# Joining three float32 words of a float64 weight: the sign by a one-operand 16-bit AND, and the last tile's output in halves

## The chip, the cores and the metric

One core of one Trainium2 chip. The metric is the device time of one execution in microseconds (us); the time before is the median of three timed runs.

## The reference

Three parts follow one another; here they are, cut to what is computed (`silu(g) = g * sigmoid(g)`):

```python
# 1: chunked state-space attention: batch 4, heads 8, sequence 768, head dim 32, state 16
for c in chunks:
    L = exp(cum[i] - cum[j]) * (i >= j)
    y = ((C @ B.T) * L) @ x + (C @ state) * exp(cum)
    state = decay_full * state + sum_j(B_j x_j * decay_from_j)
# 2: gated feed-forward, 3072 tokens x 256, inner width 1536
xn = x / sqrt(mean(x * x) + 1e-6) * rms_g
x2 = (silu(xn @ w_gate) * (xn @ w_val)) @ w_out
# 3: token-shift feed-forward, inner width 1024
xk = mu_k * x2 + (1 - mu_k) * x2_prev;  xr = mu_r * x2 + (1 - mu_r) * x2_prev
out = sigmoid(xr @ w_r) * (relu(xk @ w_k) ** 2 @ w_v)
```

The weights come as float64. The kernel does the matrix products with float32r operands in two parts: a rounded high part and the residual, three matmuls for one product.

## The kernel before, in words

The 768 positions are cut into six tiles of 128; with four batches a tile is 512 columns (T = 512). Tile t goes through attention of chunk t, then the normalization, then `ffn1` (twelve units u of 128 inner columns), then `mix`, then `ffn2` (eight units). The stages of neighbouring tiles are interleaved by `hook`: during `ffn1` of tile t (kind "ab") the attention of chunk t + 1 is put between the units, its decay exponentials (`exp_e`, for chunks 0 and 1 on ScalarE) or scans (`e_scan` L410, VectorE) before them; during `ffn2` of tile t - 1 (kind "cd") the normalization of chunk t + 1.

`mm3` (L623) issues three matmuls into one PSUM bank: high weight and high x, low weight and high x, high weight and low x. `split` (L126) makes the two parts of an activation: a cast on ScalarE (L128) and a subtraction on VectorE (L131). In `ffn1` a unit is g, v (L641, L644), a silu on ScalarE (L655), the product hf on VectorE (L656), its split, and two units later `contract` into two accumulators, one for each half of 128 output channels.

**Weights.** 27 pieces (`wjobs`) of 128 x 512 float64 are loaded two at a time into a staging buffer `wst` (two buffers, L238, SP queue) and converted by `convert` (L245), for two pieces in 1024 columns (the last one alone, 512): fourteen steps. A float64 lies there as two 32-bit words, low `lo` and high `hi`. ScalarE scales the high word, read as float32, into `t` (L257), and turns the low word into its top three bits as a number from 0 to 7, in place (L258). VectorE clamps `t` (L262). Then come the two joins in `merge`, each with two operands: `hi = (t AND sign) OR lo` (L267), and `t = (t << 3) OR hi` (L269). `parts` casts `t` to the high part on ScalarE (L278) and subtracts for the low one on VectorE (L279). The first two steps run after the normalization of chunk 0 in program order, the others when `need` asks for them: in `ffn1` of tile 0 by the list NEED, then one a unit in tile 1.

**The end.** `ffn2` contracts unit u three units late (`contract`, L705, both halves m for each unit), so after the gate's matmuls `rps` and its sigmoid three units are left (L736), then for each half one product (L739) and one store of 256 KB (L740).

**The order.** The program order is not the issue order. `arrange` (L1129) takes all instructions, prices each (`price`, L998: a VectorE instruction with two operands at 1.03 ns a column, with one at 0.52, plus 75), finds what depends on what by address ranges (`region` L979, `meet` L991, with a marker for the even or odd place of a stride of two), and simulates a list schedule: an engine that is free takes the ready instruction that stands first in the program. That order is then fixed on each engine, the SP and ScalarE queues' DMA issues among them.

Of the kernel before, what the change touches and what calls it, by code (L numbers as in the profile page):

```python
# [8 lines left out]

F32 = mybir.dt.float32  # L10
F32R = mybir.dt.float32r
BF16 = mybir.dt.bfloat16
I32, U32 = mybir.dt.int32, mybir.dt.uint32
AF = mybir.ActivationFunctionType
ALU = mybir.AluOpType
# [3 lines left out]
NC = S // P  # L19
DM, DFF, DFF2 = 256, 1536, 1024  # L20
NU, NK = DFF // P, DFF2 // P
T = NB * P
# [27 lines left out]
TOP3 = (2.0 ** -29 * (1 - 2.0 ** -12), 7.5 * 2.0 ** -12 - 0.5)  # L50
# [17 lines left out]
def tile_kernel(ctx: ExitStack, tc, a_c, x_t, B_t, B_s, C_s, B_p, C_p, C_h, kc,  # L68
                w_gate, w_val, w_out, w_k, w_v, w_r, out):
    nc = tc.nc  # L70
# [21 lines left out]
    def t2(name, dt=F32, tag="t2"):  # L92
        return rp.tile([P, T], dt, tag=tag, bufs=5, name=name)

    def t4(name, dt=F32, tag="wt"):
        return rp.tile([P, 2, T], dt, tag=tag, bufs=1, name=name)
# [3 lines left out]
    def pair(tag, name, dt=F32R):  # L100
        return rp.tile([P, 2, T], dt, tag=tag, bufs=pair_bufs[tag], name=name)
# [4 lines left out]
    def f32(ap):  # L106
        return ap.bitcast(F32)
# [29 lines left out]
    RE = 2 * 2 * NB  # L137
    starts = t2("starts", BF16)[:RE].rearrange("p (h i) -> p h i", h=4)
    nc.gpsimd.memset(starts, 1.0)
# [3 lines left out]
    for base in (0, -32):  # L143
        nc.gpsimd.affine_select(out=pick, in_=f32(pick), pattern=[[-1, RE]], base=base, channel_multiplier=1,
                                compare_op=ALU.not_equal, fill=1.0)
    eye = wp.tile([P, P], BF16, name="eye")
    before = wp.tile([P, P], BF16, name="before")
    nc.gpsimd.memset(eye, 0.0)
# [4 lines left out]
                            compare_op=ALU.is_ge, fill=-30000.0)  # L153
    cmask = wp.tile([P, NH * P], BF16, name="cmask")
    nc.gpsimd.memset(cmask, 0.0)
    nc.gpsimd.affine_select(out=cmask, in_=cmask, pattern=[[0, NH], [1, P]], base=0, channel_multiplier=-1,
                            compare_op=ALU.not_equal, fill=1.0)
    lmask = wp.tile([P, NB, P + 1], BF16, name="lmask")
    nc.gpsimd.memset(lmask, 0.0)
# [41 lines left out]
    def wpair(k, m, name):  # L201
        return (wp.tile([P, k, m], F32R, name=name + "h"), wp.tile([P, k, m], F32R, name=name + "l"))

    wg, wv, wo = wpair(2, DFF, "wg"), wpair(2, DFF, "wv"), wpair(NU, DM, "wo")
    wk, wvv, wr = wpair(2, DFF2, "wk"), wpair(NK, DM, "wvv"), wpair(2, DM, "wr")
# [10 lines left out]
    for q in range(NU // 2):  # L216
        s, k2 = slice(2 * P * q, 2 * P * (q + 1)), slice(2 * q, 2 * q + 2)
# [10 lines left out]
    staged = {}  # L228
# [15 lines left out]

    def convert(j):  # L245
        js = range(j, min(j + 2, len(wjobs)))
        st = staged.pop(j // 2).rearrange("p i a b -> p (i a b)").rearrange("p (n w) -> p n w", w=2)
        t2w = t4("wt2", I32, "Cs" if j % 4 else "wt")
        tw = t2w.rearrange("p i n -> p (i n)")

        def part(i):
            s = slice(0, T * len(js)) if i is None else slice(T * i, T * i + T)
            return st[:, s, 0], st[:, s, 1], tw[:, s]

        def magnitude(i=None):
            lo, hi, t = part(i)
            nc.scalar.activation(out=t.bitcast(F32), in_=hi.bitcast(F32), func=AF.Copy, scale=2.0 ** -112)  # L257
            nc.scalar.activation(out=lo, in_=lo.bitcast(U32), func=AF.Copy, scale=TOP3[0], bias=TOP3[1])  # L258

        def move(i=None):  # L260
            lo, hi, t = part(i)
            nc.vector.tensor_scalar(out=t.bitcast(F32), in0=t.bitcast(F32), scalar1=-W_MAX, scalar2=W_MAX,  # L262
                                    op0=ALU.max, op1=ALU.min)

        def merge(i=None):
            lo, hi, t = part(i)
            nc.vector.scalar_tensor_tensor(out=hi, in0=t, scalar=-0x80000000, in1=lo,  # L267
                                           op0=ALU.bitwise_and, op1=ALU.bitwise_or)
            nc.vector.scalar_tensor_tensor(out=t, in0=t, scalar=3, in1=hi,  # L269
                                           op0=ALU.logical_shift_left, op1=ALU.bitwise_or)  # L270

        def parts(i=None):
            for n, k in enumerate(js):
                if i not in (None, n):
                    continue
                _, wh, wl = wjobs[k]
                t = t2w[:, n, :].rearrange("p (k m) -> p k m", k=2).bitcast(F32)
                nc.scalar.copy(wh, t)  # L278
                (vec_e if k in SUB_DVE else pool_e).tensor_tensor(out=wl, in0=t, in1=f32(wh), op=ALU.subtract)  # L279

        return magnitude, move, merge, parts

    done = [0, 0]
# [418 lines left out]
    def ffn2(t, hook):  # L702
        acc = [None, None]
        hs = {}

        def contract(u):
            h = hs.pop(u)
            for m in range(2):
                if u == 0:
                    acc[m] = patt.tile([P, T], F32, tag="at", name=f"v_{m}")  # L710
                mm3(acc[m], wvv, u, m, h, u == 0, u == NK - 1)

        for u in range(NK):
            hook("cd", u)
            kp = pmm.tile([P, T], F32, tag="mm", name="kp")
            for k in range(2):
                mm3(kp, wk, k, u, xm[t, 0, k], k == 0, k == 1)
            if u == 0:
                hook("cd2", u)
            rl, k2 = t2("rl"), t2("k2")  # L720
            nc.scalar.activation(out=rl, in_=kp, func=AF.Relu)  # L721
            nc.vector.tensor_mul(k2, rl, rl)  # L722
            hs[u] = pair("hl", "h2")
            split(hs[u], k2, act_e, vec_e)
            if u >= 3:
                contract(u - 3)
        hook("cd", NK)
        rs = []
        for m in range(2):
            rps = pmm.tile([P, T], F32, tag="mm", name="rps")  # L730
            for k in range(2):
                mm3(rps, wr, k, m, xm[t, 1, k], k == 0, k == 1)
            r = t2("r")
            tabled(out=r, in_=rps, func=AF.Sigmoid)
            rs.append(r)
        for u in range(NK - 3, NK):  # L736
            contract(u)
        for m in range(2):
            nc.vector.tensor_mul(rs[m], rs[m], acc[m])  # L739
            nc.sync.dma_start(out=out[t, m], in_=rs[m])  # L740


    full, cols = slice(0, T), (slice(0, T // 2), slice(T // 2, T))
# [67 lines left out]
    for t in range(NC):  # L811
        c, e = t + 1, t + 2
# [127 lines left out]
class Order:  # L940
# [37 lines left out]
    @staticmethod  # L978
    def region(a, slots):  # L979
        ap = a.bass_ap  # L980
        steps = list(ap.ap)
        row = max(1, steps[0][0])
        at = ap.offset % row
        if ap.tensor.name.startswith("la_") or slots.get(ap.tensor.name, ("",))[0] == "PSUM":
            return ap.tensor.name, (0, 1 << 40, 0, P, None)
        end = at + sum((c - 1) * max(s, 0) for s, c in steps[1:]) + 1
        size = 2 if ap.tensor.dtype == BF16 else 4
        return ap.tensor.name, (at * size, end * size, ap.offset // row, ap.offset // row + steps[0][1],
                                at % 2 if steps[-1][0] == 2 else None)

# [186 lines left out]
```

## Time and profile before

| | |
|---|---|
| median of three timed runs | 533.19 us (532.39 to 533.31) |
| the profiled execution | 534.13 us |
| its span, first to last instruction | 532.1 us |
| mean granted TensorE clock | 0.994 of full speed |
| busy, TensorE matmul | 517.5 us (97%) |
| busy, VectorE | 402.7 us (76%) |
| busy, ScalarE | 314.7 us (59%) |
| busy, GpSimd | 14.3 us (3%) |

The page gives the busy time of each engine over the whole span. A table by stage gives the same for a stretch, with the granted clock. A group of instructions gives the mean duration of one and the time that the engine idled just before them, with what ended that idle time. L267 is line 267 of the kernel. PE is TensorE's matmuls, PEld its weight loads, DVE is VectorE, ACT ScalarE, POOL GpSimd, SP the engine that issues most transfers (SPq and ACTq are the queues of issues).

### The profile page before, as it was taken

To read this page: it belongs to the slowest core of one execution; us is meant where nothing else is said; L and a number is where in the kernel's file an instruction comes from. 1 tells how busy PE (TensorE), PEld (TensorE's weight loads), DVE (VectorE), ACT (ScalarE), POOL (GpSimd) and SP (SyncE) were. 2 spreads that over 40 slices of the span, in tenths; PEclk is the share of its full clock that TensorE was granted. 3 is DMA by queue.
4 is the path that set the end of the run, shared out by engine and by line. 5 is a ranking of instruction groups with operands and counts; after the bars stand their busy time and mean duration, and the time that the engine had idled before them with its cause. 6 is when DMAs were issued, how large, how long until landed. Compare 5 with 4: busy or idle time off the path is not lost.

```text
span 532.1 us, 7505 instructions
## 1 busy us (share of the span) xinstructions
PE 517.5 (97%) x2831; PEld 414.7 (78%) x2831; DVE 402.7 (76%) x640; ACT 314.7 (59%) x546; POOL 14.3 (3%) x30
## 2 busy tenths in 40 slices
PE   9969989999989999999999999999999999999997
PEld 6646767778768888888788888888888888888885
DVE  5798999999999986587996598986455863335772
ACT  4998768845736774445774445774437663245552
POOL 4000000000002000001000001000000000000000
PEclk9988999999999999999999999999999999999999
DMA  8543565534334011314011314011000010000001
GB/s 256 196 158 112 172 216 183 173 94 149 99 109 149 20 41 41 118 62 176 22 39 42 119 58 160 1 41 39 1 0 2 2 39 1 0 0 1 21 21 39
DMA packets 21635, 42.20 MB, mean 79 GB/s; under 512 B 2064, under 2 KB 4880, under 8 KB 21600
## 3 DMA queue, kind: packets, MB, share of 16 engines
q1 hardware_dynamic: 19296, 33.34, 18.8%
q10 hardware_dynamic: 2304, 8.39, 4.7%
q8 instruction: 22, 0.36, 0.3%
q14 instruction: 13, 0.11, 0.1%
HBM read 38.38 MB, written 3.34 MB: 78 GB/s over the span
## 4 chain that ended last, share of the span: by engine, by line
PE 89%; DVE 2%; ACT 2%; DMA 1%; issue 1%; ACTq 0%; DVEq 0%
PE v L625 10%; PE v L627 10%; PE v L626 10%; PE g L625 7%; PE g L626 6%; PE x L627 6%; PE g L627 6%; PE x L625 6%; PE x L626 6%; PE kp L625 4%; PE kp L627 4%; PE kp L626 4%; PE y L494 2%; PE y L523 1%; PE sc L462 1%; PE rps L626 1%
## 5 line engine op out<-in xcount | busy, mean ns | idle before, releaser
L656 DVE TENSOR_TENSOR hf<-sl,v 128x512 f32<-128x512 f32 x72 | 49.2, 683 | 48.8 <-PE v L627 45.2
L128 ACT CAST h<-hf 128x512 fp32r<-128x512 f32 x72 | 44.5, 618 | 62.7 <-DVE hf L656 58.5
L116 ACT ACTIVATE sl<-g 128x512 f32<-128x512 f32 x72 | 42.7, 593 | 44.5 <-PE g L627 44.4
L131 DVE TENSOR_TENSOR h<-hf,h 128x512 fp32r<-128x512 f32 x72 | 50.4, 702 | 23.4 <-ACT h L128 23.3
L625 PE MATMUL g<-xn,wgh 128*128 128x512 f32 x144 | 58.4, 409 | 1.5 <-ACT sl L116 0.8
L625 PE MATMUL x<-h,woh 128*128 128x512 f32 x144 | 56.5, 393 | 0.8 <-ACT h L128 0.8
L626 PE MATMUL g<-xn,wgl 128*128 128x512 f32 x144 | 57.2, 397 | 0.0
L625 PE MATMUL v<-xn,wvh 128*128 128x512 f32 x144 | 56.4, 395 | 0.6 <-ACT sl L116 0.6
L627 PE MATMUL g<-xn,wgh 128*128 128x512 f32 x144 | 56.9, 395 | 0.0
L626 PE MATMUL v<-xn,wvl 128*128 128x512 f32 x144 | 56.5, 392 | 0.0
L627 PE MATMUL v<-xn,wvh 128*128 128x512 f32 x144 | 56.3, 391 | 0.0
L627 PE MATMUL x<-h,woh 128*128 128x512 f32 x144 | 55.8, 391 | 0.4 <-DVE h L131 0.4
L626 PE MATMUL x<-h,wol 128*128 128x512 f32 x144 | 56.1, 389 | 0.0
L722 DVE TENSOR_TENSOR k<-rl 128x512 f32<-128x512 f32 x48 | 35.2, 738 | 15.1 <-ACT rl L721 14.9
L128 ACT CAST h<-k 128x512 fp32r<-128x512 f32 x48 | 29.7, 620 | 16.0 <-DVE k L722 15.9
L131 DVE TENSOR_TENSOR h<-k,h 128x512 fp32r<-128x512 f32 x48 | 32.7, 685 | 7.4 <-ACT h L128 7.0
L721 ACT ACTIVATE rl<-kp 128x512 f32<-128x512 f32 x48 | 28.4, 595 | 16.2 <-PE kp L627 15.8
L625 PE MATMUL kp<-xm,wkh 128*128 128x512 f32 x96 | 37.8, 393 | 0.0
L627 PE MATMUL v<-h,wvvh 128*128 128x512 f32 x96 | 37.5, 390 | 0.0
L627 PE MATMUL kp<-xm,wkh 128*128 128x512 f32 x96 | 37.5, 390 | 0.0
L625 PE MATMUL v<-h,wvvh 128*128 128x512 f32 x96 | 37.4, 389 | 0.0
L626 PE MATMUL v<-h,wvvl 128*128 128x512 f32 x96 | 37.4, 389 | 0.0
(135 smaller groups left out, 1040.7 us busy)
## 6 DMA issues: line engine op xcount, KB each, us to landing
E<-la_r ACTq DMA_DIRECT2D x16, 512.0 KB
x<-in_x_t SPq DMA_DIRECT2D x6, 512.0 KB
wst<-in_w_gate SPq DMA_DIRECT2D x6, 512.0 KB
wst<-in_w_val SPq DMA_DIRECT2D x6, 512.0 KB
wst<-in_w_out SPq DMA_DIRECT2D x6, 512.0 KB
Br<-in_B_s SPq DMA_DIRECT2D x12, 256.0 KB
Cr<-in_C_s SPq DMA_DIRECT2D x12, 256.0 KB
out<-r SPq DMA_DIRECT2D x12, 256.0 KB
```

Of the source, the lines that this page charges most:

```text
L116: ins.append(lambda: nc.scalar.activation(out=out, in_=in_, func=func, **kw))
L128: nc.scalar.copy(x[:, 0, :], src)
L131: last[0] = le.tensor_tensor(out=x[:, 1, :], in0=src, in1=f32(x[:, 0, :]), op=ALU.subtract).ins
L462: nc.tensor.matmul(bank[half][:, q * 256:(q + 1) * 256], bs[:, p, :], cs[:, p, :, :].rearrange("p a i -> p (a i)"), start=True, stop=True)
L494: nc.tensor.matmul(y[half][32 * j:32 * j + 32, at[half]:at[half] + P], x[:, b, h * D:(h + 1) * D], m[:, h, :], start=start and at[half] == ...
L523: mm = nc.tensor.matmul(y[half][:, k * P:(k + 1) * P], Sf[g, b + k].rearrange("p h d -> p (h d)"), d["Ch"][g, b + k, :], start=k == 0, sto ...
L625: nc.tensor.matmul(ps, w[0][:, k, ws], x[:, 0, :], start=first, stop=False)
L626: nc.tensor.matmul(ps, w[1][:, k, ws], x[:, 0, :], start=False, stop=False)
L627: nc.tensor.matmul(ps, w[0][:, k, ws], x[:, 1, :], start=False, stop=last)
L656: nc.vector.tensor_mul(hf, sl, v)
L721: nc.scalar.activation(out=rl, in_=kp, func=AF.Relu)
L722: nc.vector.tensor_mul(k2, rl, rl)
```

## The change

The first join is replaced. ScalarE's second pass (L258) writes its 0 to 7 as a 16-bit number over the lower half of the high word (whose value the first pass has read by then). VectorE takes the upper half of `t`, as 16-bit numbers, ANDs it with 0x8000 and writes it to the upper half of the high word: one operand and a constant. So the high word then holds sign and low bits, and the second join is as before.

In the last tile the three remaining contractions are done for half 0 of the output first, then for half 1, and half 1's product and store are cut in two of 256 columns.

The planner's `region` knows the 16-bit type.

```diff
-BF16 = mybir.dt.bfloat16
+BF16, U16 = mybir.dt.bfloat16, mybir.dt.uint16
     def convert(j):
         js = range(j, min(j + 2, len(wjobs)))
-        st = staged.pop(j // 2).rearrange("p i a b -> p (i a b)").rearrange("p (n w) -> p n w", w=2)
+        sf = staged.pop(j // 2).rearrange("p i a b -> p (i a b)")
+        st = sf.rearrange("p (n w) -> p n w", w=2)
...
+        def halves(i):
+            s = slice(0, T * len(js)) if i is None else slice(T * i, T * i + T)
+            h = sf.bitcast(U16).rearrange("p (n w) -> p n w", w=4)[:, s]
+            return h[:, :, 2], h[:, :, 3]
+
         def magnitude(i=None):
             lo, hi, t = part(i)
             nc.scalar.activation(out=t.bitcast(F32), in_=hi.bitcast(F32), func=AF.Copy, scale=2.0 ** -112)
-            nc.scalar.activation(out=lo, in_=lo.bitcast(U32), func=AF.Copy, scale=TOP3[0], bias=TOP3[1])
+            nc.scalar.activation(out=halves(i)[0], in_=lo.bitcast(U32), func=AF.Copy, scale=TOP3[0], bias=TOP3[1])
...
         def merge(i=None):
             lo, hi, t = part(i)
-            nc.vector.scalar_tensor_tensor(out=hi, in0=t, scalar=-0x80000000, in1=lo,
-                                           op0=ALU.bitwise_and, op1=ALU.bitwise_or)
+            nc.vector.tensor_scalar(out=halves(i)[1], in0=t.bitcast(U16).rearrange("p (n w) -> p n w", w=2)[:, :, 1],
+                                    scalar1=0x8000, scalar2=None, op0=ALU.bitwise_and)
             nc.vector.scalar_tensor_tensor(out=t, in0=t, scalar=3, in1=hi,
                                            op0=ALU.logical_shift_left, op1=ALU.bitwise_or)
...
-        for u in range(NK - 3, NK):
-            contract(u)
+        if t + 1 < NC:
+            for u in range(NK - 3, NK):
+                contract(u)
+        else:
+            us = [(u, hs.pop(u)) for u in range(NK - 3, NK)]
+            for m in range(2):
+                for u, h in us:
+                    mm3(acc[m], wvv, u, m, h, False, u == NK - 1)
         for m in range(2):
-            nc.vector.tensor_mul(rs[m], rs[m], acc[m])
-            nc.sync.dma_start(out=out[t, m], in_=rs[m])
+            parts = [slice(0, T)] if m == 0 or t + 1 < NC else [slice(0, T // 2), slice(T // 2, T)]
+            for c in parts:
+                nc.vector.tensor_mul(rs[m][:, c], rs[m][:, c], acc[m][:, c])
+                nc.sync.dma_start(out=out[t, m][:, c], in_=rs[m][:, c])
...
-        size = 2 if ap.tensor.dtype == BF16 else 4
+        size = 2 if ap.tensor.dtype in (BF16, U16) else 4
```

## Rows read from the trace of the kernel before

**Rows 1.** The page's busy line: busy us (share of span) and instructions.

```profile
PE 517.5 (97%) x2831; PEld 414.7 (78%) x2831; DVE 402.7 (76%) x640; ACT 314.7 (59%) x546; POOL 14.3 (3%) x30
```

**Rows 2.** The table by stage; columns as in its first line.

```profile
core 0: us, PE busy (x) PEld busy (x) DVE busy (x) ACT busy (x) POOL busy (x), PEclk, DMA share, GB/s
24.70:31.00 6.30, 1.68 (x8) 0.69 (x7) 5.88 (x14) 6.10 (x19) 0.00 (x0) 1.00 0.70 221
31.00:34.20 3.20, 3.20 (x8) 2.21 (x9) 3.20 (x7) 3.20 (x7) 0.00 (x0) 0.50 0.02 6
34.20:44.20 10.00, 8.45 (x36) 5.45 (x34) 9.96 (x16) 9.76 (x30) 0.00 (x0) 0.99 0.61 212
44.20:48.70 4.50, 4.45 (x12) 3.51 (x13) 2.67 (x5) 3.78 (x6) 0.00 (x0) 0.62 0.33 101
...
78.00:80.30 2.30, 0.88 (x6) 0.79 (x5) 2.06 (x7) 2.27 (x7) 0.00 (x0) 1.00 1.00 319
80.30:146.40 66.10, 66.06 (x424) 51.93 (x422) 65.21 (x99) 45.62 (x73) 0.11 (x1) 1.00 0.42 138
146.40:151.00 4.60, 2.88 (x11) 1.67 (x11) 4.60 (x8) 2.26 (x5) 0.00 (x0) 1.00 0.35 96
151.00:528.20 377.20, 377.19 (x1979) 310.71 (x1979) 263.82 (x422) 205.28 (x337) 7.43 (x6) 1.00 0.13 46
```

**Rows 3.** Groups by line and shape: busy us, mean ns; then L267 alone in one stage.

```profile
L412 DVE TENSOR_TENSOR_SCAN E<-E,cmask 128x1024 f32<-128x1024 f32 x16 | 36.6, 2285 | 0.9 <-DMA E<-la_r 0.9
...
L267 DVE SCALAR_TENSOR_TENSOR wst<-wt,wst 128x1024 int32<-128x1024 int32 x13 | 15.9, 1223 | 0.9 <-ACT wst L258 0.3
L269 DVE SCALAR_TENSOR_TENSOR wt<-wt,wst 128x1024 int32<-128x1024 int32 x13 | 15.9, 1221 | 0.1
L258 ACT ACTIVATE wst<-wst 128x1024 int32<-128x1024 uint32 x13 | 15.1, 1164 | 0.0
...
L262 DVE TENSOR_SCALAR wt<-wt 128x1024 f32<-128x1024 f32 x13 | 8.9, 688 | 0.5 <-ACT wt L257 0.5
...
L595 DVE TENSOR_SCALAR ms<-ss 128x256 f32<-128x256 f32 x2 | 0.8, 418 | 0.0
...
48.70:146.40 97.70, 12.91 (x11) 1.00 0.45 148
```

**Rows 4.** The timeline of the opening: start us, us, VectorE, then ScalarE.

```profile
24.52 1.23 DVE L267 SCALAR_TENSOR_TENSOR wst<-wt,wst 128x1024 int32<-128x1024 int32 x1
25.67 0.42 DVE L595 TENSOR_SCALAR ms<-ss 128x256 f32<-128x256 f32 x1
26.29 0.42 DVE L601 SCALAR_TENSOR_TENSOR nw<-nw,ms 128x256 f32<-128x256 f32 x1 [0.21 <-ACT nw L116]
...
32.68 1.22 DVE L269 SCALAR_TENSOR_TENSOR wt<-wt,wst 128x1024 int32<-128x1024 int32 x1
...
43.60 0.60 ACT L116 ACTIVATE sl<-g 128x512 f32<-128x512 f32 x1
```

**Rows 5.** The timeline of ScalarE around 78 us.

```profile
77.04 1.16 ACT L257 ACTIVATE wt<-wst 128x1024 f32<-128x1024 f32 x1 [2.44 <-PE y L494]
...
78.08 0.63 ACT L535 COPY yT<-y 128x256 f32<-128x256 f32 x2
```

**Rows 6.** From the chain that ended last, then the timeline, 136 to 151 us.

```profile
136.10 5.40 DMA Br<-in_B_s
...
141.53 0.73 ACT L421 ACTIVATE Bs<-Br,k_sb 128x512 fp32r<-128x512 f32 x1 [2.11 <-DMA Br<-in_B_s]
...
145.35 2.28 DVE L412 TENSOR_TENSOR_SCAN E<-E,cmask 128x1024 f32<-128x1024 f32 x1
...
149.51 0.50 PE L625 MATMUL x<-h,woh 128*128 128x512 f32 x1 [0.77 <-ACT h L128]
```

**Rows 7.** The end: chain, then the transfers' GB/s in 40 slices of 528.0 to 532.1.

```profile
528.32 0.69 DVE r L739
...
GB/s 0 0 0 0 0 0 0 0 0 0 0 140 360 360 460 380 340 340 360 380 420 380 380 380 360 80 0 0 0 0 0 0 0 0 0 0 0 0 0 0
```

## The prediction

> **What bounds the kernel now.** I read the busy line first: TensorE works 97% of the span, VectorE 76% [rows 1]. So VectorE time is worth something only where TensorE waits, and the table by stage finds those places. From 151.0 us to the last matmul TensorE is busy 377.19 of 377.20 us [rows 2]; nothing that VectorE saves there can show. Ahead of that TensorE idles in three places. [...] Around 79 us: 1.42 us. From 146.4 to 151.0: 1.72 us [rows 2]. Time won in one of these shifts all that follows, and reaches the end in full, since the long stage has no slack to swallow it. The last 3.9 us hold the two closing products, two transfers and the landing.
>
> The profiled execution took 534.13 us with a span of 532.1; the median of the timed runs, 533.19, is 0.94 lower. I work out differences inside the span and take them off the median. A measurement of this kernel tells some 0.2%, 1.07 us, from no change.
>
> **The AND.** The first of the two joins in `merge`, a two-operand instruction of 1223 ns (13 times at 1024 columns, once at 512), becomes a one-operand AND over 1024 16-bit numbers, read at every second and written at every fourth 16-bit place. The trace has no such instruction. The nearest row is the clamp in `move`: one operand, a constant, the same 1024 columns, 688 ns against 1223 [rows 3]. It is packed and 32 bits wide, the new one is neither. From below I take half of that, 344 ns, for a doubled rate once more; from above the dearest instruction over 1024 columns in the trace, the scan at 2285 ns [rows 3]. I take 688, because the stride has shown no price so far: the first join reads and writes every second 32-bit word and takes 1223 ns, the second one writes packed words and takes 1221 [rows 3].
>
> [...]
>
> Saved at 688 ns: 13 x 0.535 + half of it = 7.2 us of VectorE. Where: eleven of the fourteen instructions (ten whole, one half) lie between 48.7 and 146.4 us [rows 3], the other three before; the eleven save 5.6 us in a stretch where VectorE is busy 65.21 of 66.10 us [rows 2].
>
> **The low bits and the order.** ScalarE's second pass writes 16-bit numbers over the lower half of the high word in place of the low word: as many columns, so I leave it at its 1164 ns [rows 3]. From below a narrower number is no fewer columns, so nothing is gained; from above, doubled, eleven passes would be 12.8 us more from 48.7 us on, and from 80.3 to 146.4 alone ScalarE idles 20.5 us [rows 2], so it would still not be the bound. It must now follow the first pass, which reads that word; the planner can no longer swap the two. The AND no longer reads the low bits; it waits for the clamp alone, unless the two halves are taken as overlapping, then it waits as before (0.3 us in all [rows 3]). The planner prices the AND at about half the join, and hands out work by program order to whichever engine it thinks free; all five engines' order can therefore move, the weights' loads on the SP queue too, since the staging buffer comes free with the last join. The last join keeps its price.
>
> **146.4 to 151.0 us.** The largest of TensorE's waits is 0.77 us, for the cast of h, which follows hf [rows 6]. Behind it stands a jam on VectorE, busy 4.60 of 4.60 us [rows 2]: residuals of xm, a scan of 2.28 us begun at 145.35, then hf [rows 6]. With 5.6 us of work less ahead, VectorE comes to the last weights, the mixing and the scans earlier. One cause stays: ScalarE sits 2.11 us for Br until 141.53, a transfer that TensorE's last read of the buffer released at 136.1 [rows 6]. I credit 1.2 of the 1.72 us.
>
> **Around 79 us.** The copies of yT start at 78.08 because ScalarE first runs a weight's pass from 77.04, itself held, by the profile, until TensorE's y [rows 5]. Whether the weight's pass moves ahead is the planner's choice; earlier joins let it come earlier. I credit 0.4 of 1.42.
>
> **The opening.** ScalarE is the bound: it works 6.10 of 6.30, 3.20 of 3.20 and 9.76 of 10.00 us [rows 2], with the exponentials of chunk 1 that must end before a table load and the first silu at 43.60, for which TensorE waits [rows 4]. VectorE's saving of 1.6 us (three ANDs) does not shorten that. I credit nothing; it can go either way (rivals).
>
> **The end.** The last tile's three contractions run all of half 0 first, so acc[0] is ready nine matmuls earlier, and its product and transfer leave the end. Half 1 is multiplied and stored in two halves. Now the second product starts at 528.32 and takes 0.69, so its transfer goes out at about 529.0; both transfers pass between 529.1 and 530.7 [rows 7]. Two half products at some 0.42 us (the 256-column row, 418 ns [rows 3]), overlapped by 0.04, end 0.07 us later than one of 0.68; the last transfer has 128 KB less, 0.35 us at 380 GB/s. Gain 0.28, bounds -0.1 (only the fixed part counts) and +0.45 (no queueing behind half 0 either). SP has one issue more; it falls between the two half products.
>
> **Sum.** 1.2 + 0.4 + 0 + 0.3 = 1.9 us: 533.19 - 1.9 = 531.3.
>
> **The rivals.**
> A, the forecast, 531.3, chance 0.42.
> B, the opening shrinks too: if the exponentials end 0.4 us sooner, TensorE's wait for the first silu shrinks and the clock need not fall; the stretch of 4.5 us at 0.62 alone costs 1.7 us [rows 2]. For it: VectorE is busy 5.88 of 6.30 us there. Against: ScalarE is busier. 531.3 - 1.7 - 0.4 = 529.2, chance 0.12.
> C, VectorE's time was hidden: ScalarE's wait for Br, not VectorE, sets the hole at 146 us, freed VectorE slots fill with scans, and only the end gains. Here belongs also that the halves count as overlapping. 532.9, chance 0.24.
> D, slower: the planner fills a hole it opens itself. In the opening the join at 24.52 ends just as the mean's instruction (0.42 us) starts at 25.67, and 0.21 us later the chain to xn goes on at 26.29; the second join of that weight only runs at 32.68 [rows 4]. With the first join 0.53 us shorter, VectorE is free from about 25.55 to 26.29, and the planner, which leaves no engine idle, can put the second join, 1.22 us, there. The chain to the first matmul then slips 0.5 us, or up to 1.2 where the same happens to the casts on ScalarE, and the stretch at half clock grows with it. It decides when the second join is ready before 26.3 in the planner's reckoning. For it: the 1.2 us are ready work. Against: TensorE waits for the silu at 43.6 anyway. 533.19 + 1.2 = 534.4, chance 0.14.
> E, the 16-bit stride has no doubled rate. At 1.22 us nothing is saved but the end: 532.9, chance 0.05. Dearer than the join, up to 2285 ns: eleven times up to 1.06 us more on a VectorE that is full, so 536 to 544, chance 0.03.
>
> **Chances and range.** Faster by over 0.2%: A and B, 0.54. Within: C and the first of E, 0.29. Slower: D and the dear E, 0.17. The range runs from 529.0, just under B, to 534.5, just over D: it leaves out the dear E and the outer half of B and D. A alone would lie between 529.7 (all of both holes) and 532.4.
>
> **What would show it.** The AND near 0.69 us in the groups by shape, and 14 of them; VectorE's busy sum down by about 7 us; the stage after 146 us without a wait of TensorE over 0.3 us; the copies of yT close behind TensorE's y at 77; the last stretch 0.3 us shorter, with two stores of 128 KB. I am wrong if the AND takes 1.2 us or more, if TensorE's idle time before 151 us stays at some 9 us although VectorE has 7 us less to do, or if the first silu moves by over 1 us either way.

## The result and the profile after

The changed kernel takes 540.87 us (median of 4 runs, 540.40 to 541.22) against 533.25 us (4 runs, 532.39 to 533.46) for the kernel before, measured beside it: a ratio of 1.0145, 95% interval 1.0128 to 1.0163. It is 7.6 us slower, where 531.3 us was forecast, and outside the range. The profiled execution took 540.4 us with a span of 538.4 us.

The page's busy line of the changed kernel, as in [rows 1]:

```profile
PE 520.4 (97%) x2831; PEld 415.7 (77%) x2831; DVE 404.6 (75%) x641; ACT 332.7 (62%) x546; POOL 12.7 (2%) x30
```

Its groups by line and shape, as in [rows 3] (busy us, mean ns, then the idle time ahead and what ended it). L264 and L265 are ScalarE's two passes, L274 the AND, L276 the join that is left.

```profile
L265 ACT ACTIVATE wst<-wst 128x1024 uint16<-128x1024 uint32 x13 | 32.9, 2533 | 0.2
L274 DVE TENSOR_SCALAR wst<-wt 128x1024 uint16<-128x1024 uint16 x13 | 17.5, 1343 | 0.1
L276 DVE SCALAR_TENSOR_TENSOR wt<-wt,wst 128x1024 int32<-128x1024 int32 x13 | 15.9, 1225 | 0.6 <-ACT wst L265 0.4
L264 ACT ACTIVATE wt<-wst 128x1024 f32<-128x1024 f32 x13 | 15.1, 1159 | 1.8 <-PE y L501 0.9 <-DMA wst<-in_w_v 0.9
...
L265 ACT ACTIVATE wst<-wst 128x512 uint16<-128x512 uint32 x1 | 1.4, 1372 | 0.0
L274 DVE TENSOR_SCALAR wst<-wt 128x512 uint16<-128x512 uint16 x1 | 0.8, 753 | 0.0
```

Two durations are new; the other passes over the weights kept theirs (the first pass takes 1159 ns, the join that is left 1225). ScalarE's second pass, which had taken 1164 ns [rows 3], takes 2533 ns: 13 x 1.37 us are 17.8 us more of ScalarE, and the busy line shows 332.7 us against 314.7 [rows 1]. The AND takes 1343 ns, dearer than the join of 1223 ns that it replaces [rows 3]; VectorE's sum rose by 1.9 us where it was to fall by 7. With twice the columns, the pass takes 1161 ns more (2533 - 1372) and the AND 590 ns more (1343 - 753): 2.27 and 1.15 ns per column, so it is the column that is dear, not the instruction.

The table by stage shows where that lands; the columns are those of [rows 2], the first four stretches too, the others are cut by the changed kernel's own holes.

```profile
24.70:31.00 6.30, 2.17 (x9) 1.25 (x10) 4.81 (x11) 6.17 (x12) 0.00 (x0) 0.93 0.73 214
31.00:34.20 3.20, 1.89 (x4) 1.06 (x4) 3.17 (x9) 3.12 (x11) 0.00 (x0) 0.50 0.02 5
34.20:44.20 10.00, 8.95 (x33) 6.03 (x32) 9.58 (x15) 9.97 (x23) 0.00 (x0) 0.86 0.55 192
44.20:48.70 4.50, 2.79 (x10) 1.17 (x8) 2.73 (x5) 4.47 (x12) 0.00 (x0) 0.84 0.21 59
48.70:54.00 5.30, 5.26 (x12) 4.12 (x13) 4.86 (x7) 5.30 (x6) 0.00 (x0) 0.50 0.23 74
...
60.00:80.00 20.00, 18.99 (x88) 13.79 (x86) 18.70 (x27) 16.68 (x19) 0.00 (x0) 1.00 0.49 165
...
146.40:165.00 18.60, 16.72 (x129) 12.56 (x128) 18.46 (x28) 10.05 (x19) 0.00 (x0) 1.00 0.13 50
165.00:534.30 369.30, 369.30 (x1902) 305.10 (x1900) 255.96 (x412) 203.36 (x333) 5.81 (x6) 1.00 0.14 45
```

ScalarE now works through the opening almost without a gap (9.97 of 10.00, 4.47 of 4.50, 5.30 of 5.30 us) and TensorE waits for it: 2.79 us busy of 4.50 ahead of the first silu, then 5.3 us at a granted clock of 0.50 of full speed. From 165 us on TensorE is busy without a gap (369.30 of 369.30 us), as before [rows 2].

ScalarE's own timeline in the opening and around 64 to 74 us (start us, us) shows what stands in the queue. Behind each of the passes of 2.5 us shown here stands a cast or a silu that starts 2.2 to 2.3 us after it.

```profile
24.43 2.49 ACT L265 ACTIVATE wst<-wst 128x1024 uint16<-128x1024 uint32 x1
26.67 0.67 ACT L285 CAST wgh<-wt 128x512 fp32r<-128x512 f32 x1
...
35.06 2.52 ACT L265 ACTIVATE wst<-wst 128x1024 uint16<-128x1024 uint32 x1
37.33 0.68 ACT L285 CAST woh<-wt 128x512 fp32r<-128x512 f32 x1
...
48.09 0.60 ACT L116 ACTIVATE sl<-g 128x512 f32<-128x512 f32 x1
...
64.32 2.55 ACT L265 ACTIVATE wst<-wst 128x1024 uint16<-128x1024 uint32 x1
66.58 0.71 ACT L116 ACTIVATE sl<-g 128x512 f32<-128x512 f32 x1
...
71.11 2.54 ACT L265 ACTIVATE wst<-wst 128x1024 uint16<-128x1024 uint32 x1
73.39 0.70 ACT L116 ACTIVATE sl<-g 128x512 f32<-128x512 f32 x1
```

The first silu, at 43.60 us before [rows 4], starts at 48.09. The two longest of TensorE's waits from 60 to 165 us (total us, times, longest) name ScalarE as well:

```profile
PE v L632 <- ACT wvh L285: 1.1, 2, 0.7
PE v L632 <- ACT sl L116: 1.1, 1, 1.1
```

Set against the end: the last matmul starts at 534.27 us (527.82 before), so 6.45 us are lost ahead of it; from there to the end of the span it is 4.09 us, against 4.26.

### The profile page after: what moved, and what is told of

Its sections match the earlier page's. It is cut to its first block, busy times and chain, and to the rows that moved or that the text cites. A ratio compares the mean times of both kernels' runs of the same rounds, so it can differ in the third digit from the quotient of the medians.

```text
span 538.4 us, 7487 instructions
## 1 busy us (share of the span) xinstructions
PE 520.4 (97%) x2831; PEld 415.7 (77%) x2831; DVE 404.6 (75%) x641; ACT 332.7 (62%) x546; POOL 12.7 (2%) x30
## 4 chain that ended last, share of the span: by engine, by line
PE 74%; ACT 11%; DVE 10%; issue 3%; DMA 1%; ACTq 0%; DVEq 0%; SPq 0%
PE v L633 8%; PE v L634 8%; PE v L632 8%; PE x L634 5%; PE g L632 5%; PE x L633 5%; PE x L632 5%; PE g L633 4%; PE g L634 4%; PE kp L632 4%; PE kp L634 4%; PE kp L633 4%; ACT wst L265 3%; ACT E L116 3%; ACT wt L264 2%
## 5 line engine op out<-in xcount | busy, mean ns | idle before, releaser
L632 PE MATMUL v<-xn,wvh 128*128 128x512 f32 x144 | 57.0, 397 | 2.2 <-ACT wvh L285 1.1
L634 PE MATMUL v<-xn,wvh 128*128 128x512 f32 x144 | 57.0, 396 | 0.0
L419 DVE TENSOR_TENSOR_SCAN E<-E,cmask 128x1024 f32<-128x1024 f32 x16 | 37.7, 2357 | 1.2 <-DMA E<-la_r 1.2
L632 PE MATMUL v<-h,wvvh 128*128 128x512 f32 x96 | 37.4, 389 | 0.0
```

The lines of the kernel that those rows point to most:

```text
L419: nc.vector.tensor_tensor_scan(out=e, data0=e, data1=cmask, initial=0.0, op0=ALU.mult, op1=ALU.max)
L632: nc.tensor.matmul(ps, w[0][:, k, ws], x[:, 0, :], start=first, stop=False)
L634: nc.tensor.matmul(ps, w[0][:, k, ws], x[:, 1, :], start=False, stop=last)
```

## The experiments

Three things change at once: the durations, the order that the planner makes of them, and the end. The first four runs take them apart. Where it is said below that two kernels have one order, every engine's instructions stand in the same sequence.

**e1_low32: the changed kernel, ScalarE's pass as a 32-bit one.** It writes the whole high word; the AND then overwrites the upper half. The order is that of the changed kernel.

```
-            nc.scalar.activation(out=halves(i)[0], in_=lo.bitcast(U32), ...)
+            nc.scalar.activation(out=hi, in_=lo.bitcast(U32), ...)
```

> The changed kernel with one edit: ScalarE's second pass writes its 0 to 7 as a 32-bit number over the whole high word, and the AND then sets the sign in its upper half. Same results, and every engine's order is that of the changed kernel. Theory (ScalarE's price): the second pass went from 1164 to 2533 ns, and in the opening, where ScalarE is the bound, that is the loss; here it is back near 1.16 us and the time falls from 540.9 to 533 to 535. Rival (order): the planner's new order is the loss, the passes are hidden; the time stays at 539 to 541. Second rival (VectorE's price): the AND at 1343 ns instead of 1223 is the loss; it stays at 539 to 541 as well, with the AND still near 1.34 us.

Measured: 534.92 us (6 runs) against 533.30, ratio 1.0028 (1.0017 to 1.0039). The pass is back at 1165 ns, the AND stays dear. The groups by shape of this kernel:

```profile
L274 DVE TENSOR_SCALAR wst<-wt 128x1024 uint16<-128x1024 uint16 x13 | 17.4, 1338 | 1.5 <-ACT wst L265 1.4
...
L265 ACT ACTIVATE wst<-wst 128x1024 int32<-128x1024 uint32 x13 | 15.1, 1165 | 0.2
```

So the write of ScalarE's pass alone makes 6.0 of the 7.6 us (540.87 - 534.92). Since the order is the same, the two traces can be laid over each other, instruction by instruction. The starts of the first silu and of some matmuls (numbered in TensorE's order, which is the same in both), in us:

```
                    changed   e1_low32   later by
first silu            48.09      45.29       2.80
matmul 250            55.42      52.97       2.45
matmul 330            74.48      70.68       3.80
matmul 360            80.35      75.81       4.54
matmul 600           115.92     110.77       5.15
matmul 800           145.36     139.89       5.47
matmul 850           156.53     150.73       5.80
last matmul          534.27     528.48       5.79
```

The loss grows in steps. About 2.5 us arise in the opening, 2.1 more by 80 us, and 1.3 more between 80 and 157 us, part of it at TensorE's second wait for the cast wvh, near 97 us (0.4 us), and part at its wait for a silu, near 154 us (1.1 us, 0.8 in e1_low32). What comes after adds nothing.

**e2_order: the kernel before, in the changed kernel's order.** The code is that of before; only the planner is told that the first join costs half. Up to the last tile the order is then that of the changed kernel.

```
+        if e == DVE_ and kind != 'InstTensorTensor' and aps and aps[0].bass_ap.tensor.name.startswith('wst'):
+            return 75 + 0.52 * n, 75.0, True
```

> The kernel before, with the planner alone told that the first join costs 0.52 ns a column, as it reckons the AND. No instruction changes; each engine's order becomes that of the changed kernel (but for its last tile). Theory (ScalarE's price): about 533, at most 1 us from the kernel before. Rival (order): 538 to 541, the loss without any 16-bit write. If it lies between, the difference to 533.2 is the order's part.

Measured: 533.77 us (10 runs) against 533.30, ratio 1.0017 (1.0004 to 1.0030). The order, which the planner makes for a cheap AND, costs 0.5 us by itself by the medians, 0.2 to 1.6 us by the interval. In the profiled executions its first silu starts at 45.82 us, 2.22 later than in the kernel before, and its last matmul at 527.51, 0.31 earlier (that execution of the kernel before was 0.9 us above its median). So between two orders the first silu is no measure. The same 231 matmuls stand ahead of it in both, but ScalarE has one more of the weights' passes ahead of it (at 41.26 us, 1.18 us), work that is then done. Between e2_order and e1_low32 lies what remains of the loss, some 0.6 to 1.2 us: ANDs of 1338 ns in place of joins of 1222, and their wait. The two intervals overlap, but both are taken against the same runs of the kernel before. The runs themselves say that this part is probably real: all six of e1_low32 (534.61 to 535.20) lie above eight of the ten of e2_order, and the two traces, of one order, are 0.97 us apart at the last matmul.

**e3_weights and e4_tail: the end.** e3_weights is the changed kernel with the old end, e4_tail the kernel before with the new one.

```
-        if t + 1 < NC:
-            for u in range(NK - 3, NK):
-                contract(u)
-        else:
...
+        for u in range(NK - 3, NK):
+            contract(u)
```

> The changed kernel with the last tile's end as before: the weights' part alone. Theory: the end is worth 0.1 to 0.3 us (the stretch from the start of the last matmul to the end of the span went from 4.28 to 4.13 us in the two profiles), so 541.0 to 541.2. Rival (the end is where the loss is): below 537.

> The kernel before with the new end of the last tile alone. Theory: 0.1 to 0.3 us faster than before, 532.9 to 533.1; with the prediction's 0.28. Rival: two smaller stores with rows of half the length cost as much as they save, no difference or slower by up to 0.3 us.

Measured: e3_weights 540.86 us (4 runs), ratio 1.0139 (1.0126 to 1.0152); e4_tail 533.45 us (12 runs) against 533.30, ratio 0.9999 (0.9985 to 1.0012). In the profiles, the stretch from the last matmul to the end of the span is 4.08 to 4.09 us with the new end and 4.26 with the old (the 4.28 and 4.13 of the expectation rest on spans rounded to 0.1 us). 0.17 us is what the profiles show; the times can't tell it from nothing. The loss is in the weights.

**e5_forms: what makes these writes dear.** Fourteen forms, two of each, run behind the kernel's last unit, where nothing else is left to do (the time of this run, 556.32 us, means nothing). In the code, q4 is every fourth 16-bit place of 8-byte pairs, q2 every second 32-bit word, w2 every second 16-bit place, w1 packed 16-bit, W packed 32-bit; the names in the rows are fq for the first two and fw for the rest.

```
+            act(out=q2[:, :, 0], in_=lo, **kw)          # L759
+            act(out=q2[:, :, 1], in_=lo, **kw)
+            act(out=q4[:, :, 2], in_=lo, **kw)          # L761
+            act(out=w2[:, :, 0], in_=lo, **kw)
+            act(out=w1, in_=lo, **kw)
+            act(out=W, in_=lo, **kw)
+            ts(out=q4[:, :, 3], in0=w2[:, :, 1], ...)   # L765
+            ts(out=w2[:, :, 1], in0=w2[:, :, 1], ...)
+            ts(out=w1, in0=q4[:, :, 3], ...)            # L767
+            ts(out=q4[:, :, 3], in0=w1, ...)
+            ts(out=w1, in0=w1, ...)                     # L769
+            ts(out=W, in0=W, ...)
+            ts(out=q2[:, :, 1], in0=W, ...)             # L771
+            ts(out=q2[:, :, 1], in0=q2[:, :, 0], ...)
```

> The kernel before, and behind its last unit fourteen forms of the two instructions over 1024 columns, each twice, on scratch tiles that nothing else reads; its own time means nothing, the durations by line do. ScalarE's second pass, from every second 32-bit word: to 32-bit in place (known, 1.16 us), to 32-bit at the other word, to 16-bit at every fourth place (known, 2.53), to 16-bit at every second place, to 16-bit packed, to 32-bit packed. Theory (a 16-bit number that fills half of a word costs a second access): the two strided 16-bit forms at 2.5 us, the packed one and all 32-bit ones at 1.0 to 1.2. Rival (the 16-bit type itself): all three 16-bit forms at 2.5. Rival (the step of 8 bytes together with 16 bits): only the step of four at 2.5, the step of two in between. VectorE's one-operand AND: 16-bit from step 2 to step 4 (known, 1.34), step 2 to step 2, step 4 to packed, packed to step 4, packed to packed; 32-bit packed to packed, packed to step 2, step 2 to step 2. Theory (the write of half words costs, and reads are free): forms that write strided 16-bit at 1.3 us, the packed 16-bit write at 0.69 or less, all 32-bit ones at 0.69. Rival (the 16-bit type loses the doubled rate at any step): all 16-bit ones at 1.2 to 1.35. Rival (the step loses it): the 32-bit forms with a step at 1.2 too.

The groups by shape of that stretch (busy us, mean ns):

```profile
L761 ACT ACTIVATE fq<-fq 128x1024 uint16<-128x1024 uint32 x2 | 5.0, 2494 | 0.0
L762 ACT ACTIVATE fw<-fq 128x1024 uint16<-128x1024 uint32 x2 | 2.7, 1366 | 0.0
L768 DVE TENSOR_SCALAR fq<-fw 128x1024 uint16<-128x1024 uint16 x2 | 2.6, 1304 | 0.1
L765 DVE TENSOR_SCALAR fq<-fw 128x1024 uint16<-128x1024 uint16 x2 | 2.6, 1304 | 11.1 <-ACT fw L764 11.1
L760 ACT ACTIVATE fq<-fq 128x1024 int32<-128x1024 uint32 x2 | 2.2, 1122 | 0.0
...
L763 ACT ACTIVATE fw<-fq 128x1024 uint16<-128x1024 uint32 x2 | 2.2, 1107 | 0.1
...
L766 DVE TENSOR_SCALAR fw<-fw 128x1024 uint16<-128x1024 uint16 x2 | 1.5, 735 | 0.1
L771 DVE TENSOR_SCALAR fq<-fw 128x1024 int32<-128x1024 int32 x2 | 1.4, 696 | 0.1
L772 DVE TENSOR_SCALAR fq<-fq 128x1024 int32<-128x1024 int32 x2 | 1.4, 695 | 0.1
L767 DVE TENSOR_SCALAR fw<-fq 128x1024 uint16<-128x1024 uint16 x2 | 1.4, 694 | 0.1
...
L769 DVE TENSOR_SCALAR fw<-fw 128x1024 uint16<-128x1024 uint16 x2 | 0.9, 427 | 0.1
```

Neither factor alone does it. A 16-bit write is not dear as such (1107 ns packed on ScalarE, 427 on VectorE), and at every second place it takes little more than 32-bit words do (1366 and 735). A step of 8 bytes is not dear as such either: 32-bit words 8 bytes apart are written in 1122 and 696 ns. Reading 16-bit numbers 8 bytes apart and writing them packed takes VectorE 694 ns: more than the 427 of packed to packed, but no more than 32-bit words. And with the dear write it makes no difference whether VectorE reads packed numbers (L768) or every second place (L765). What is dear is a 16-bit write with 8 bytes from one to the next: 2494 ns on ScalarE and 1304 on VectorE, about twice what 32-bit words at that spacing take on the same engine (1122 and 696). No form writes 32-bit words at every fourth place, so whether it is the 8 bytes or the step of four items that counts stays open. Why it is so inside the chip no run here shows.

**e7_act16: the kernel before with ScalarE's 16-bit pass alone.** The join keeps two operands: the high word, masked with 7, since the low bits now lie there, and `t`, taken whole (the selection of the sign bit is left out). The second pass must then follow the first, so the order is neither that of the kernel before nor that of the changed one; up to the end it is that of e9_packed_ord, below.

```
-            nc.scalar.activation(out=lo, in_=lo.bitcast(U32), ...)
+            nc.scalar.activation(out=lo16(i), in_=lo.bitcast(U32), ...)
...
-            nc.vector.scalar_tensor_tensor(out=hi, in0=t, scalar=-0x80000000, in1=lo,
+            nc.vector.scalar_tensor_tensor(out=hi, in0=hi, scalar=7, in1=t,
```

> The kernel before with ScalarE's second pass writing 16-bit numbers into the lower half of the high word, and a first join of the old kind and price that reads the high word, masks it with 7 and takes t as its second operand (so the weights' low bits come out otherwise; the sign's selection is left out). So ScalarE's 16-bit pass alone, without the AND, with an order of the planner's own. Theory (ScalarE's price alone makes the loss): 538 to 541, with the second pass at 2.5 us and both joins at 1.22. Rival (both 16-bit instructions are needed for the loss): 533 to 536.

Measured: 543.74 us (4 runs) against 533.33, ratio 1.0197 (1.0174 to 1.0220). The groups by shape:

```profile
L263 ACT ACTIVATE wst<-wst 128x1024 uint16<-128x1024 uint32 x13 | 33.0, 2537 | 0.3
L272 DVE SCALAR_TENSOR_TENSOR wst<-wst,wt 128x1024 int32<-128x1024 int32 x13 | 15.9, 1226 | 7.2 <-ACT wst L263 7.0
```

Without any AND, the pass brings the loss, and more of it: now VectorE's join waits for it as well (7.0 us in all, 0.3 before [rows 3]). Its order is another, so the size can't be set against the changed kernel. It can against e9_packed_ord, which has the same order, a pass of 1160 ns and an AND of 772 in place of the join: 533.42 us. Some 10 us lie between the two, and the cheaper AND explains about 2 of them if it is worth as much as in the other order (e8_packed). So the dear pass makes a loss in this order too, and a larger one.

**e6_priced: the planner told the truth.** The same kernel as the changed one, with the measured prices.

```
+        if e == ACT_ and half:
+            return 206 + 2.28 * n, 100.0, False
+        if e == DVE_ and half:
+            return 75 + 1.2 * n, 75.0, True
```

> The changed kernel with the planner told what the two 16-bit instructions measured (206 + 2.28 n and 75 + 1.2 n ns for n columns). The instructions stay; only the order moves. Theory (ScalarE's time in the opening is the loss, the order does little): 539 to 541. Rival (a wrong price list let the long pass stand ahead of the exponentials; told the truth, the planner hides it): 534 to 537.

Measured: 549.84 us (4 runs, 546.82 to 550.60) against 533.33, ratio 1.0296 (1.0259 to 1.0334): nine us worse than with the wrong prices. The table by stage shows TensorE's gaps in two places of this order, 24.7 to 60 and 110 to 165 us:

```profile
24.70:60.00 35.30, 23.71 (x90) 14.96 (x88) 29.95 (x49) 33.21 (x65) 0.00 (x0) 0.90 0.44 147
60.00:110.00 50.00, 47.93 (x307) 35.45 (x306) 47.98 (x68) 41.04 (x50) 0.10 (x1) 0.99 0.52 176
110.00:165.00 55.00, 48.64 (x272) 38.95 (x272) 49.58 (x75) 34.37 (x53) 0.00 (x0) 0.88 0.28 96
```

TensorE is busy 23.71 of 35.30 us and 48.64 of 55.00; the kernel before has 29.08 and 53.24 in the same stretches of its trace. So telling the planner the true prices does not win the loss back, and an order alone can cost more than the whole loss. Why its order for true prices is worse than its order for wrong ones stays open, and so does whether some other order would hide the dear passes.

**e10_early16 and e11_late16: where the pass hurts.** In the changed kernel, and in its order, the 16-bit pass is kept in the first three conversions only (which lie ahead of the first silu), or in all the others only; the rest write 32 bits as in e1_low32.

```
-  out=halves(i)[0]
+  out=halves(i)[0] if j < 6 else hi      (e10_early16)
+  out=halves(i)[0] if j >= 6 else hi     (e11_late16)
```

> The changed kernel with ScalarE's second pass in 16 bits in the first three conversions only (those ahead of the first silu) and in 32 bits over the whole high word in the other eleven. Orders as in the changed kernel. Between 534.9 (none in 16 bits) and 540.9 (all). Theory (ScalarE binds the opening alone, and the three passes push the first silu): three times 1.37 us, 539 to 540, the first silu near 48 us. Rival (the loss is spread over all fourteen): 536.0 to 536.5.

> The complement: the first three conversions in 32 bits, the other eleven in 16. Theory (behind the first silu ScalarE has room): 535 to 536.5, the first silu near 45.5 us. Rival (the late passes delay casts and silus for which TensorE waits): 538 or more.

Measured, both against 532.54: e10_early16 537.05 us (4 runs), ratio 1.0091 (1.0066 to 1.0117); e11_late16 538.39 us (4 runs), ratio 1.0112 (1.0087 to 1.0136). Over e1_low32's 1.0028 that is 0.63% for three early passes and 0.84% for the late ones. By the profiled executions the early ones cost 1.8 us of span and the late ones 4.2 (534.4 and 536.8 against 532.6). Both theories are refuted: the early passes cost less than expected, the late ones more, and it is not the opening alone that matters. In e10_early16 the first silu starts at 48.04 us, as late as in the changed kernel, but of these 2.75 us against e1_low32 only 1.82 arrive at the last matmul (530.30 against 528.48). A stretch from 60 us on in the table by stage, first in e11_late16:

```profile
60.00:75.00 15.00, 13.45 (x56) 9.29 (x55) 13.85 (x20) 13.24 (x16) 0.00 (x0) 0.89 0.50 160
```

then in e1_low32, whose order is the same:

```profile
60.00:75.00 15.00, 15.00 (x72) 11.52 (x71) 14.51 (x22) 10.91 (x15) 0.00 (x0) 1.00 0.56 187
```

and TensorE's waits in e11_late16 from 48 to 80 us:

```profile
PE v L632 <- ACT wvh L285: 1.5, 1, 1.5
```

ScalarE is busy 13.24 of 15.00 us, so it has 1.76 us free, and still TensorE waits 1.5 us for one cast. That cast starts at 67.59 us, 2.1 later than in e1_low32 (65.51); ahead of it in ScalarE's order stand two silus and, at 61.83 us, a pass of 2.5 us. The granted clock of the stretch is 0.89 behind that wait and 1.00 without it. A mean share of 88% did not hide the pass. The two halves are not exact shares of the loss, since the changed kernel's own clock stays at 1.00 from 60 to 80 us.

**e8_packed: the same idea without the dear write.** ScalarE writes 32-bit words packed into the front of the staging buffer; the AND then writes their upper halves (16 bits at every second place), and the join reads packed words. The order is that of the changed kernel.

```
+        def low(i):
+            return sf[:, :T * len(js)]
+        def upper(v):
+            return v.bitcast(U16).rearrange("p (n w) -> p n w", w=2)[:, :, 1]
-            nc.scalar.activation(out=halves(i)[0], in_=lo.bitcast(U32), ...)
+            nc.scalar.activation(out=low(i), in_=lo.bitcast(U32), ...)
...
+            nc.vector.tensor_scalar(out=upper(low(i)), in0=upper(t), scalar1=0x8000, ...)
-            nc.vector.scalar_tensor_tensor(out=t, in0=t, scalar=3, in1=hi,
+            nc.vector.scalar_tensor_tensor(out=t, in0=t, scalar=3, in1=low(i),
```

> The changed kernel with the same work in layouts that cost nothing extra by the forms measured alone: ScalarE's second pass writes 32-bit words packed into the front of the staging buffer (about 1.12 us), the AND reads t's upper halves and writes the packed words' upper halves, step 2 to step 2 (about 0.74 us), the join reads the packed words. Same results; every engine's order is exactly that of the changed kernel. This makes the prediction's premise true: VectorE has 13 x 0.49 us less than before. Theory A (the prediction's sum was right but for the two prices): 531 to 532.5, 1 to 2 us under before. Theory B (VectorE's time is hidden, and the new order costs what the join-only run showed, 0.5 us): 533 to 534. If it stays above 536, the two prices weren't the loss.

Measured: 531.65 us (12 runs, 530.74 to 532.42) against 533.00 (23 runs), ratio 0.9977 (0.9967 to 0.9986). It beats both kernels. Its groups by shape:

```profile
L267 ACT ACTIVATE wst<-wst 128x1024 int32<-128x1024 uint32 x13 | 15.1, 1161 | 0.2
L276 DVE TENSOR_SCALAR wst<-wt 128x1024 uint16<-128x1024 uint16 x13 | 10.1, 776 | 2.3 <-ACT wst L267 2.2
L277 DVE SCALAR_TENSOR_TENSOR wt<-wt,wst 128x1024 int32<-128x1024 int32 x13 | 15.9, 1220 | 0.1
```

and its table by stage around the two holes that the prediction wanted to close:

```profile
48.70:60.00 11.30, 11.30 (x48) 9.15 (x46) 10.30 (x15) 8.97 (x13) 0.00 (x0) 0.94 0.51 163
60.00:80.00 20.00, 20.00 (x140) 15.38 (x140) 18.23 (x29) 13.71 (x23) 0.00 (x0) 1.00 0.58 169
80.00:146.40 66.40, 66.40 (x424) 52.11 (x423) 65.14 (x102) 46.29 (x72) 0.10 (x1) 1.00 0.44 144
146.40:165.00 18.60, 18.01 (x125) 14.08 (x125) 17.90 (x26) 8.99 (x14) 2.72 (x2) 1.00 0.47 149
```

TensorE has no gap from 48.7 to 146.4 us; the 1.42 us around 79 us [rows 2] are gone, and of the gaps behind 146.4 us 0.59 are left.

Not all of this is the cheaper AND. e2_order has the same order up to the end, with joins of 1222 ns. Its rows, then two of the kernel before:

```profile
24.70:60.00 35.30, 27.85 (x100) 19.85 (x100) 32.38 (x53) 30.15 (x68) 0.00 (x0) 0.85 0.46 152
78.00:80.30 2.30, 2.29 (x11) 1.63 (x10) 2.23 (x7) 2.27 (x6) 0.00 (x0) 1.00 0.98 328
146.40:165.00 18.60, 17.32 (x121) 13.18 (x120) 17.15 (x25) 9.93 (x16) 1.42 (x2) 1.00 0.46 131
...
24.70:60.00 35.30, 29.08 (x112) 20.23 (x112) 32.59 (x54) 30.27 (x68) 0.00 (x0) 0.90 0.46 151
146.40:165.00 18.60, 16.88 (x119) 13.08 (x119) 18.53 (x28) 8.58 (x15) 2.58 (x2) 1.00 0.48 149
```

The hole around 79 us closes by the order alone (2.29 of 2.30 us), and the order loses time in the opening in return. What the cheaper AND gives shows between these two kernels of one order: 531.65 us against 533.77, 0.40% by the ratios. Laid over each other, e8_packed is ahead by 0.38 us at matmul 310, 1.07 at 525 and 840, 2.06 at 850 and 2.08 at the last one.

**e9_packed_ord: the same, with the AND priced at 1.03 ns per column in the planner.** Every instruction is that of e8_packed, the order is another.

```
+        if e == DVE_ and kind != 'InstTensorTensor' and aps and aps[0].bass_ap.tensor.name.startswith('wst'):
+            return 75 + 1.03 * n, 75.0, True
```

> The same as the packed version, with the planner told that the AND costs as much as the old join (1.03 ns a column). Only the order differs. Theory (the order moves the opening by about 1 us either way): 532 to 535. Rival (with no engine's time added, the order is neutral): within 0.5 us of the packed version.

Measured: 533.42 us (10 runs) against 533.00, ratio 1.0007 (0.9989 to 1.0024), no difference to the kernel before that can be told. The two orders of the same work lie 1.8 us apart, more than the whole gain. So the gain of e8_packed hangs on its order too.

## Why the prediction was wrong

**What bounds the kernel: right.** The loss is made where the prediction looked for gains, ahead of the long stage. From 165 us on TensorE has no gap in either kernel (369.30 of 369.30 us in the changed one; the one before in the last line of [rows 2]), and what is lost by 157 us arrives at the end whole (5.80 us at matmul 850, 5.79 at the last, against e1_low32).

**The low bits: the step that failed.** The prediction left ScalarE's second pass at 1164 ns, because "a narrower number is no fewer columns". It took 2533 ns. The columns are as many, but each costs twice as much. This step had the upper bound in hand, doubled passes, and threw it away with "so it would still not be the bound": it held 12.8 us of more work against 20.5 us that ScalarE idles from 80.3 to 146.4 us, a sum over a stage in which only 0.9 of the 5.8 us arose (4.54 us late at matmul 360, 5.47 at 800). 4.5 us are lost by 80 us, 2.5 of them in the opening, and there the prediction itself had read ScalarE at 6.10 of 6.30 us, 3.20 of 3.20 and 9.76 of 10.00 [rows 2] and called it the bound of the opening. Doubling the passes in that stretch would have put the first silu some 3 x 1.16 us later, and made a rival at 536.7 us: the measured lateness of the first silu against the same order is 2.80 us (e1_low32), though the early passes by themselves cost only 1.8 us at the end (e10_early16). Later, a pass of 2.5 us some places ahead of a cast was enough for a wait of 1.5 us, though ScalarE had room on the mean (busy 13.24 of 15.00 us, e11_late16).

**The AND: mis-sized.** 688 ns were taken, 1343 measured; the bounds of 344 to 2285 held it. The reason given, that a stride had shown no price, rested on a join that writes 32-bit words 8 bytes apart. That is right for those (695 ns against 694 packed, e5_forms) and says nothing of 16-bit numbers at the same spacing. The two steps failed for one cause, the 16-bit write at every fourth place. Of the loss it is the small part: the ANDs and their order together are the 1.6 us between the kernel before and e1_low32.

**The wait of the AND: right.** It waits for ScalarE nowhere (0.1 us idle in all); the remaining join took over the wait, 0.4 us.

**The holes: the total near, its makeup right in part.** With an AND of 776 ns and a pass of 1161 (e8_packed) the forecast of 1.9 us less compares with 1.35 us by the medians, 0.7 to 1.8 us by the interval. Of the 1.72 us behind 146.4 us, 1.13 are gained (credited 1.2), and between matmul 840 and 850 e8_packed wins 1.0 us over e2_order, so the cheaper AND is worth something near that here: this credit was sound. The hole around 79 us closes whole (1.42 us, credited 0.4), but by the planner's order, which the prediction had named, and not by VectorE's shorter work, since it closes in e2_order too. The opening, credited with nothing, gives part of it back: TensorE is busy 28.19 us from 24.7 to 60 us where the kernel before has 29.08. That a hole closed by the order and an opening hurt by it nearly cancel is luck, and e9_packed_ord, with the same instructions in another order, gains nothing that can be told.

**The end: too small to tell.** 0.17 us in the profiles against 0.28 forecast, within its bounds; the times show none of it.

**The rivals.** None held. E had the right cause, the 16-bit stride, but named only VectorE; its dear case, 536 to 544 us, covers the result for another reason, at a chance of 0.03. D's mechanism, ready work put ahead of the mean's instruction, came in a weaker form: in e2_order it is a subtraction (wgl, 0.68 us at 25.43), not the second join, and the mean's instruction starts at 26.03 us where it was 25.67; the whole order costs 0.5 us by the medians. C's premise is refuted: between e2_order and e8_packed VectorE's shorter work is worth 2.1 us.

**The tests that were named.** The AND of 1.2 us or more, and the first silu over 1 us late, were both listed as signs of a wrong prediction, and both came. The silu only counts between kernels of one order: in e2_order it is 2.2 us late with no loss at the last matmul.

## What to carry to other kernels

Price an access pattern by item width and spacing together, and for each engine that the edit touches: here, over 1024 columns, 16-bit numbers written 8 bytes apart took about twice as long as 32-bit words at that spacing on both (2494 against 1122 ns on ScalarE, 1304 against 696 on VectorE), while 16-bit numbers 4 bytes apart took little more than those words (1366 and 735 ns). When an upper bound doubles an instruction, lay it into the stretches in which TensorE waits for that engine's next result, not against the idle sum of a long stage. Lateness is read from matmuls of two kernels in one order; a silu that stood behind long passes was late by itself (2.75 us in e10_early16, of which 1.82 arrived at the last matmul). And where an edit changes what a planner makes of the order, run the old code in the new order once, to keep the two apart.

## What the runs showed of the hardware that was not expected

- The doubled price is that of the write: 2494 ns on ScalarE and 1304 ns on VectorE for 1024 columns, while reading at the same spacing and writing packed takes VectorE 694 ns, as long as 32-bit words (694 to 696), though packed to packed takes 427.
- The clock is not a property of the order alone: over the span, 23 runs of the kernel before show mean granted clocks from 0.987 to 0.997. Up to its end e4_tail has the order of the kernel before; in the profiled execution of before, the granted clock falls a second time from 44.2 to 48.7 us (0.62 on the mean [rows 2]), in e4_tail's it does not (0.997 over the span against 0.994), and its first output product starts at 187.51 us, 2.1 us ahead of 189.62 (0.7 us of it are there at the first silu, 42.92 against 43.60). The runs of the kernel before spread from 530.86 to 535.32 us, so a difference of 1 us takes many runs to tell.
